# Hedgehog linear attention and an MLP on one core: which engine issues the loads of w1's and w2's later parts, and when

## The chip, the cores and the metric

The kernel runs on one core of one Trainium2 chip. A core has a matrix engine (TensorE, PE in the profile; its weight loads are PEld), a vector engine (VectorE, DVE), an activation engine (ScalarE, ACT), a general engine (GpSimd, POOL) and a small engine that here only issues transfers (SyncE, SP). Each engine works through its own instructions in order. Transfers (DMAs) can be issued by SP, ACT or POOL and are carried out by 16 DMA engines that all of them share. The metric is the device time of one execution in microseconds (us); lower is better.

## The reference

The program is a transformer block of two parts over x of shape 1 x 2048 x 576: linear attention with 32 heads of width 18, then an MLP with 4608 hidden units. All tensors are bf16.

```python
x = A_x
h  = x + _A_ref(_layernorm(x, axis=-1), A_wqkv, A_w_phi, A_wo)
h2 = h + _B_ref(_layernorm(h, axis=-1), B_w1, B_b1, B_w2, B_b2)

# _A_ref: q, k, v = x @ wqkv, by heads
pq = jnp.einsum("bhsd,hdf->bhsf", q, w_phi)      # pk the same from k
phi_q = jnp.concatenate([_softmax(pq, axis=-1), _softmax(-pq, axis=-1)], axis=-1)
kv = jnp.einsum("bhsf,bhsd->bhfd", phi_k, v)
z  = jnp.einsum("bhsf->bhf", phi_k)
num = jnp.einsum("bhqf,bhfd->bhqd", phi_q, kv)
den = jnp.einsum("bhqf,bhf->bhq", phi_q, z)[..., None] + 1e-6
o = num / den                                     # then joined by heads, @ wo

# _B_ref: layernorm once more, then
h = _gelu(jnp.einsum("bsd,df->bsf", y, w1) + b1)
return jnp.einsum("bsf,fd->bsd", h, w2) + b2
```

## The kernel before

The 2048 rows are 16 tiles of 128, taken as 8 pairs (0 to 7). The order of all instructions on all five engines is written out by hand: the calls in the code, from `warm(6)` on, are each engine's order. There is no planner.

**First half.** Keys, values and queries are projected, exponentials of keys are taken on ACT, summed and weighed on DVE and POOL, and `sums(p, a)` (L728) adds every tile's key-value products into one PSUM accumulator, `acc_kv`. The last call is `sums(6, 0)`. After it the tiles `vals` and `exk` (values and weighed key exponentials) are dead, and the memory that they held is given, by `close_keys`, to two weight tiles: w1's second part and w2's first part. So no load of these may start before the last of the sums.

**Weights of the MLP.** w1 (576 x 4608) is held in two parts, one for the steps 0 to 8 of the loop over the hidden layer and one for the steps 9 to 17; `load_w1(q, n, eng)` (L759) loads one sixth of part q, 64 partitions of 3 x 1152 values, 432 KB. w2 (4608 x 576) is held in two parts of 18 blocks of 128 rows; `load_w2(h, n, eng)` (L767) loads one sixth of part h, three blocks, 128 partitions of 3 x 576 values, 432 KB too. The last argument is the engine that issues the load: `syn` is SP, `sca` is ACT, `pool` is POOL. w2's second part lies where the query and value weights were, and may be loaded once the last query product (`query_mm(7, 0)`, L485) is done. w1's first part is loaded much earlier and isn't touched by the change. So 18 loads of 432 KB, 7.96 MB, belong to this place: w1's second part, w2's first part, w2's second part.

**Second half.** Behind the sums the remaining queries are projected, and pair 0 goes through the attention's end: `combine_mm` (query features times `kvm`, L818), `divide` (L831 and L832), a turn by TensorE, the product with wo (`residual_mm`, L868), the layernorms and another turn. Then `first_block` begins. `up` (L1326 on PE, gelu L1348 on ACT) computes the hidden layer of pair 0 in 18 steps, one step giving two blocks of 128 hidden units; steps 0 to 8 read w1's first part, steps 9 to 17 its second. `down` (L1371) multiplies the hidden blocks with w2: for each tile and column half 36 matmuls, j = 0 to 35, counted over the block by k. Even j read w2's first part and odd j the second: matmul j reads block (j - 1) / 2 of the second part, so its sixth number 3 is read first at j = 19, number 4 at j = 25 and number 5 at j = 31.

**What is woven into the first block.** While PE computes `up` for pair 0, POOL and DVE prepare the query features of pair 1: `norm_q(1, i)` sums and weighs them (POOL, L674 and L684) into the two halves of the tile `padded`, and `turn_q(1)` (L713) turns each half into the tile `phit` by a DMA transpose that SP issues. `leave(1)` stands in `down` ahead of matmul k = 2: its `combine_mm` for the two tiles of pair 1 (L818) reads the two halves of `phit`. `norm_q(2, i)` writes into `padded` again and so waits for these transposes.

**Who issues what before the change.** Of w1's second part POOL issues three sixths and SP three; of w2's first part SP issues all six; both are spread from the end of the sums to the end of the written-out list. The six sixths of w2's second part are issued by ACT, one in every second step of `up` (steps 1, 3, 5, 7, 9, 11), each between two gelus. Every DMA that SP or ACT issues also waits, by the program's semaphores, until the one that used the same of eight semaphores before it has landed.

```python
rise = up(0, 1, {
    2 * n + 1: lambda n=n: load_w2(1, n, sca) for n in range(6)
}, 1)
```

Of the kernel before, what the change touches and what calls it, by code (L numbers as in the profile page):

```python
# [47 lines left out]
def kernel(  # L48
# [39 lines left out]
    def take(key):  # L88
        taken[key] = vacant.pop(0)
        return homes[taken[key]][:, :]  # L90

    def leave_home(key):
        vacant.append(taken.pop(key))
# [49 lines left out]
    def region(at, n):  # L143
        return shared[:, at : at + n]
# [214 lines left out]
    pool, vec, syn, sca = nc.gpsimd, nc.vector, nc.sync, nc.scalar  # L359
# [185 lines left out]
    def exponentials(key, dst, p, i):  # L545
        rows = dst[:, :, :].rearrange("p a (h s f) -> p a h s f", s=2, f=DH)
        for s in range(2):
            nc.scalar.activation(  # L548
                rows[:, :, i * HH : (i + 1) * HH, s, :],
                flight[key, p, i][:, :, 0:HALF].rearrange("p a (h f) -> p a h f", f=DH),  # L550
                AF.Exp, scale=1.0 - 2.0 * s,
            )
        give("two", (key, p, i))
# [43 lines left out]
    def query_mm(p, i):  # L597
        features("q", wqp, p, i, CROSSED)

    def query_exp(p, i):  # L600
        if p not in phiq:
            phiq[p] = take(("phiq", p)).rearrange("p (a f) -> p a f", a=2)
        exponentials("q", phiq[p], p, i)
# [97 lines left out]
    def turn_q(p):  # L701
        if p == 0:
            whole = region(4 * PW, 2 * KW * P).rearrange("p (a w k) -> p a w k", a=2, k=P)
            phiT[p] = [whole[:, a, :, :] for a in range(2)]
        elif p in (3, 5):
            phiT[p] = [
                take(("phiT", p, a))[:, 0 : KW * P].rearrange("p (w k) -> p w k", k=P)
                for a in range(2)
            ]
        else:  # L710
            phiT[p] = [phit[:, a, :, :] for a in range(2)]
        for a in range(2):
            nc.sync.dma_start_transpose(phiT[p][a], padded[:, a, :])  # L713
        if p == 0:
            leave_home(("phiq", p))
# [39 lines left out]
    def load_w1(q, n, eng):  # L755
        if q and len(w1) == 1:
            close_keys()
        c0, half = n // 2 * 3, n % 2
        eng.dma_start(  # L759
            w1[q][half * KH : (half + 1) * KH, c0 : c0 + 3, :],  # L760
            w1v[half, :, c0 : c0 + 3, q * FF // 4 : (q + 1) * FF // 4],
        )

    def load_w2(h, n, eng):
        if not w2:
            close_keys()
        eng.dma_start(w2[h][:, 3 * n : 3 * n + 3, :], w2v[h, :, 3 * n : 3 * n + 3, :])  # L767
# [35 lines left out]
    def combine_mm(t, part=None, home=None):  # L803
        p, a = divmod(t, 2)
        if t not in products:
            if home is acc_banks:
                products[t] = home(t)
            else:
                if home:
                    whole = grab("two", ("pn", t), [P, 2, 512], FP32)  # L810
                else:
                    whole = pn_pool.tile([P, 2, 512], FP32, name="pn", tag="pn")
                products[t] = [whole[:, b, :] for b in range(2)]
        pn = products[t]
        for w in range(*((0, KW) if part is None else BANKS[part])):
            b = w // 6
            at, n = (w - BANKS[b][0]) * WV, COUNT[w] * VW
            nc.tensor.matmul(  # L818
                pn[b][:, at : at + n], phiT[p][a][:, w, :], kvm[:, w, 0:n],
                start=True, stop=True,  # L820
            )
        if part != 0 and ("phiT", p, a) in taken:
            leave_home(("phiT", p, a))
# [409 lines left out]
    sums(6, 1)  # L1233
    key_weigh(6, 1, 0, vec)
    sums(6, 0)
    load_w1(1, 0, pool)
    load_w2(0, 2, syn)
    table(0)
    query_mm(7, 1)
    query_exp(7, 1)  # L1240
    combine_mm(1, 0, two)
    table(1)
    combine_mm(1, 1, two)
    divide(1)
    combine_mm(0, 1)
    load_w1(1, 3, syn)
    load_w1(1, 1, syn)
    combine_mm(0, 0)
    query_mm(2, 1)
    query_mm(6, 1)  # L1250
    query_exp(6, 1)
    query_exp(2, 1)
    load_w2(0, 0, syn)
    divide(0)
    turn_o_mm()
    turn_o_ev(1, dve)
    turn_o_ev(0, dve)
    query_mm(3, 1)
    query_exp(3, 1)
    load_w2(0, 3, syn)  # L1260
    load_w2(0, 5, syn)
    residual_mm(0, 0, double_bank(0, 0))
    residual_add(0, 0, 0)
    residual_add(0, 0, 1)
# [2 lines left out]
    residual_add(0, 1, 0)  # L1267
    query_mm(5, 0)
    residual_stats(0, 0, 1)
    load_w1(1, 2, pool)  # L1270
    residual_stats(0, 1, 0)
    residual_add(0, 1, 1)
    query_exp(5, 0)
# [5 lines left out]
    second(1)  # L1279
    query_mm(7, 0)  # L1280
    query_exp(4, 1)
    load_w1(1, 5, syn)
    rescale(0, 0)
    rescale(0, 1)
    turn2_mm(0)
# [3 lines left out]
    copy_b1(act)  # L1289
    rescale(1, 1)  # L1290
    rescale(1, 0)
    load_w2(0, 1, syn)
    load_w1(1, 4, pool)
    load_w2(0, 4, syn)
    gelu_table()
    close_weights()
    hb_pool = side_pool("hb_pool", 1)
# [15 lines left out]
    def up(p0, n, at, first=0):  # L1313
        width = n * TB
        base = p0 % 2 * TB
        per = 2 * PW // width
        h1 = [take(("h1", p0, i)) for i in range((NM + per - 1) // per)]

        def hidden(m):
            return h1[m // per][:, m % per * width : (m % per + 1) * width]  # L1320

        def pair(ph, p_, lo, hi):
            for c in range(KC):
                for half in range(2):
                    rows = slice(half * KH, (half + 1) * KH)
                    nc.tensor.matmul(  # L1326
                        ph[half][:, lo:hi],
                        w1[p_ // 9][rows, c, p_ % 9 * P : (p_ % 9 + 1) * P],
                        ln2T[rows, c, base + lo : base + hi],
                        start=(c == 0), stop=(c == KC - 1),  # L1330
                    )

        def banks_of(p_):
            return [grab("acc", ("h", p0, p_, e), [P, 2 * TB], FP32) for e in range(2)]

        begun = [banks_of(p_) for p_ in range(first)]
        for p_ in range(first):
            pair(begun[p_], p_, 0, P)
            if p_ == 0:
                yield  # L1340
        for p_ in range(NM // 2):
            if p_ in at:
                at[p_]()
            ph = begun[p_] if p_ < first else banks_of(p_)
            pair(ph, p_, P if p_ < first else 0, width)
            for half in range(2):
                m = p_ + half * NM // 2
                nc.scalar.activation(  # L1348
                    hidden(m), ph[half][:, 0:width], AF.Gelu_apprx_tanh,
                    bias=b1col[:, m : m + 1], scale=1.0,  # L1350
                )
                give("acc", ("h", p0, p_, half))
        yield hidden

    def down(p0, n, hidden, at):
        k = 0
        for i_ in range(2 * n):
            t = 2 * p0 + i_
            hb = hb_pool.tile([P, D], FP32, name="hb", tag="hb")
            nc.gpsimd.tensor_tensor(hb[:, :], xh[:, t, :], b2bc[:, :], ALU.add)  # L1360
            ot = tt_pool.tile([P, D], BF16, name="ot", tag="ot")
            last = t == NT - 1
            for c0, c1 in ((0, 512), (512, D)) if last else ((0, HALF), (HALF, D)):
                cs = slice(c0, c1)
                po = grab("acc", ("o", t, c0), [P, c1 - c0], FP32)
                for j in range(NM):
                    m = j // 2 + j % 2 * NM // 2
                    if k in at:
                        at[k]()
                    k += 1  # L1370
                    nc.tensor.matmul(  # L1371
                        po[:, :], hidden(m)[:, i_ * P : (i_ + 1) * P], w2[m // 18][:, m % 18, cs],
                        start=(j == 0), stop=(j == NM - 1),
                    )
                nc.vector.tensor_tensor(ot[:, cs], po[:, :], hb[:, cs], ALU.add)  # L1375
                give("acc", ("o", t, c0))
                if last:
                    nc.sync.dma_start(out_v[:, t, cs], ot[:, cs])
            if not last:
                nc.sync.dma_start(out_v[:, t, :], ot[:, :])  # L1380
        for key in [key for key in taken if key[0] == "h1"]:
            leave_home(key)
# [18 lines left out]
        leave_home(("lnT", i))  # L1401

    def first_block():
        rise = up(0, 1, {
            2 * n + 1: lambda n=n: load_w2(1, n, sca) for n in range(6)
        }, 1)
        turn2_mm(1, pn_pool)
        next(rise)
        for part in range(2):
            turn2_ev(1, part, dve)  # L1410
        for q in (1, 2):
            for i in range(2):
                norm_q(q, i)
            if q == 1:
                turn_q(q)
        down(0, 1, next(rise), {
            2: lambda: (leave(1), turn_q(2)), 66: lambda: enter(1),
            96: lambda: norm_q(3, 0), 112: lambda: leave(2),
        })
# [66 lines left out]
```

## Time and profile before

| | |
|---|---|
| median of 3 executions | 392.45 us (391.16 to 393.12) |
| the profiled execution, own time | 393.02 us |
| its span, first to last instruction | 391.3 us |
| PE busy | 382.6 us, 98% of the span |
| DVE, ACT, POOL busy | 166.2, 162.1, 116.5 us |
| bytes moved by DMA | 35.35 MB |

The profiled execution's own time is 1.7 us more than its span: what lies before the first and behind the last instruction. A row of the timeline gives start, duration, engine, line, operation and tiles, how many instructions it joins (x), and, in brackets, how long the engine had been idle before it and what ended that. The trace calls both weights `w`: L759 is a load of w1, L767 one of w2. `PEq`, `SPq`, `ACTq` are the engines' sequencers, where a DMA is issued; such a row's duration is that of the issue, not of the transfer. The DMA queues are q1 (issued by SP), q10 (issued by ACT) and q0 (issued by POOL).

### The profile page before, as it was taken

Reading aid. Unit: us, or ns where it says so; the run is one execution under the profiler, and the core shown is the slowest. Engines: PE = TensorE matmul, PEld = TensorE weight load, DVE = VectorE, ACT = ScalarE, POOL = GpSimd, SP = SyncE. Lnnn points to the kernel's source line nnn. Section 1 sums busy time; section 2 is a strip of 40 time slices with the busy share of each in tenths; the row PEclk is TensorE's granted clock in tenths of the full one; section 3 lists DMA queues with packets and bytes.
Section 4 is the critical chain, followed back from the end, with each engine's and each line's share of the span. In section 5 each row is a group of like instructions: output and inputs, shape, how many; then the busy total and the mean of one; then the engine's idle time right before and its main releaser. Section 6 shows DMA issues by size and latency. Waiting matters only on the chain.

```text
span 391.3 us, 9949 instructions
## 1 busy us (share of the span) xinstructions
PE 382.6 (98%) x4353; PEld 266.7 (68%) x4354; DVE 166.2 (42%) x362; ACT 162.1 (41%) x290; POOL 116.5 (30%) x159
## 2 busy tenths in 40 slices
PE   8999999999799999999999999999999999999997
PEld 6677878789478887844457887444677764447773
DVE  6999997780249388590029322000480000000100
ACT  4998875698101850056650000666300026661000
POOL 6398995140604653144003111000131110000120
PEclk9999999999899999999999999999999999999999
DMA  7999998999636568533004743000062000000000
GB/s 201 223 206 191 196 219 176 260 256 238 136 60 91 108 106 136 103 67 59 0 2 62 91 106 53 12 1 2 2 88 65 17 17 0 2 2 0 17 31 16
DMA packets 72687, 35.35 MB, mean 90 GB/s; under 512 B 59940, under 2 KB 69860, under 8 KB 72516
## 3 DMA queue, kind: packets, MB, share of 16 engines
q1 hardware_dynamic: 68432, 28.58, 39.8%
q10 hardware_dynamic: 3876, 4.81, 5.2%
q0 software_dynamic: 336, 1.33, 1.3%
q8 instruction: 34, 0.56, 0.6%
q14 instruction: 9, 0.07, 0.1%
HBM read 16.62 MB, written 2.36 MB: 48 GB/s over the span
## 4 chain that ended last, share of the span: by engine, by line
PE 89%; DMA 3%; ACT 2%; issue 2%; DVE 2%; POOL 2%; SPq 1%; POOLq 0%
PE acc L1371 37%; PE acc L1326 31%; PE two L485 9%; PE acc L868 4%; DMA phit<-padded 3%; PE two L511 3%; PE acc_kv L728 1%; POOL padded L674 1%; ACT exk L575 1%; PE two L285 1%; PE acc_kv L276 1%; PE pn L818 1%; SPq L713 1%; DVE ob L832 1%; PE acc L818 0%
## 5 line engine op out<-in xcount | busy, mean ns | idle before, releaser
L1348 ACT ACTIVATE home<-acc,b1col 128x512 bf16<-128x512 f32 (+1 forms) x180 | 98.2, 599 | 173.4 <-PE acc L1326 170.5
L1371 PE MATMUL acc<-w,home 128*128 128x288 bf16 (+2 forms) x1151 | 144.8, 288 | 0.1
L1326 PE MATMUL acc<-shared,w 64*128 64x512 bf16 (+2 forms) x1638 | 142.1, 331 | 0.4 <-ACT home L1348 0.2
L1371 PEld LDWEIGHTS <-home 128*128 128x128 bf16 x1152 | 110.1, 98 | 33.0 <-issue 1.8
L1326 PEld LDWEIGHTS <-w 64*128 64x128 bf16 x1638 | 80.4, 94 | 61.0 <-issue 2.0
L1375 DVE TENSOR_TENSOR ot<-acc,hb 128x288 bf16<-128x288 f32 (+2 forms) x32 | 14.4, 452 | 109.0 <-PE acc L1371 99.1
L1360 POOL TENSOR_TENSOR hb<-xh,b2bc 128x576 f32<-128x576 bf16 x16 | 20.4, 1275 | 104.5 <-DVE ot L1375 104.5
L674 POOL TENSOR_TENSOR padded<-home,rq 128x540 bf16<-128x540 bf16 x32 | 34.9, 1103 | 43.4 <-DMA phit<-padded 20.9
L877 DVE TENSOR_TENSOR xh<-acc,xh 128x288 bf16<-128x288 f32 x28 | 11.4, 447 | 69.9 <-PE acc L868 69.9
L292 POOL TENSOR_TENSOR rs<-va,mhalf 128x1 f32<-128x1 f32 x16 | 8.8, 552 | 102.3 <-DVE va L290 102.3
L485 PEld LDWEIGHTS <-home 64*128 64x128 bf16 x648 | 31.2, 94 | 8.3 <-issue 0.2
L616 POOL TENSOR_TENSOR exk<-exk,rk 128x576 bf16<-128x576 bf16 x20 | 23.6, 1218 | 0.6 <-DVE rk L612 0.6
L548 ACT ACTIVATE home<-two 128x576 bf16<-128x576 f32 x24 | 13.9, 661 | 8.0 <-PE two L485 8.0
L868 PEld LDWEIGHTS <-shared 64*128 64x128 bf16 x288 | 13.8, 94 | 4.4 <-issue 0.5
L296 DVE TENSOR_SCALAR shared<-xh,mv,rs 128x576 bf16<-128x576 bf16 x32 | 16.2, 566 | 0.3 <-DMA shared<-shared 0.3
L868 PE MATMUL acc<-wo,shared 64*128 64x288 bf16 x252 | 16.3, 283 | 0.0
L610 DVE TENSOR_REDUCE sk<-exk 128x64 f32<-128x1152 bf16 x12 | 15.9, 1326 | 0.5 <-ACT exk L548 0.5
L665 DVE TENSOR_REDUCE sk<-home 128x64 f32<-128x1152 bf16 x12 | 15.7, 1310 | 0.0
L831 DVE RECIPROCAL rec<-acc 128x18 f32<-128x18 f32 (+1 forms) x14 | 3.5, 247 | 27.4 <-PE acc L818 27.4
L485 PE MATMUL two<-wqp,home 64*128 64x288 bf16 x216 | 14.4, 283 | 0.0
L485 PE MATMUL two<-wv,home 64*128 64x288 bf16 x216 | 14.4, 283 | 0.0
L548 ACT ACTIVATE exk<-two 128x576 bf16<-128x576 f32 x24 | 13.8, 659 | 1.3 <-PE two L485 1.3
(97 smaller groups left out, 266.7 us busy)
## 6 DMA issues: line engine op xcount, KB each, us to landing
w<-in_B_w_dram SPq DMA_DIRECT2D x12, 432.0 KB, 11.8
w<-in_B_w_dram ACTq DMA_DIRECT2D x9, 432.0 KB, 9.5
out_dram<-ot SPq DMA_DIRECT2D x15, 144.0 KB, 2.1
w<-in_B_w_dram POOLq DMA_DIRECT2D x3, 432.0 KB, 9.8
xh<-in_A_x_dram SPq DMA_DIRECT2D x2, 576.0 KB
xh<-in_A_x_dram SPq DMA_DIRECT2D x3, 288.0 KB, 4.0
wo<-in_A_wo_dram SPq DMA_DIRECT2D x1, 648.0 KB, 5.9
wo<-in_A_wo_dram ACTq DMA_DIRECT2D x1, 648.0 KB, 11.4
```

The source lines that it names most:

```text
L296: nc.vector.tensor_scalar(dst, src, mv[:, i, 0:1], rs[:, i : i + 1], ALU.subtract, ALU.mult)
L485: nc.tensor.matmul(dst[:, a, 0:HALF], lhs[rows, c, :], w[rows, slot, i * HALF : (i + 1) * HALF], start=(n == 0), stop=(n == KC - 1),)
L548: nc.scalar.activation(rows[:, :, i * HH : (i + 1) * HH, s, :], flight[key, p, i][:, :, 0:HALF].rearrange("p a (h f) -> p a h f", f=DH), A ...
L610: nc.vector.tensor_reduce(sk[:, :, :], part_of(dst, i), AX.X, ALU.add)
L616: eng.tensor_tensor(part, part, flight["r" + key, p, i][:, a, :].rearrange("p (h o) -> p h o", o=1).to_broadcast([P, NH, DH]), ALU.mult,)
L665: nc.vector.tensor_reduce(sk[:, :, :], part_of(phiq[p], i), AX.X, ALU.add)
L674: eng.tensor_tensor(padded[:, a, g0 * P : (g0 + 5) * P].rearrange("p (g k) -> p g k", k=P)[:, :, 0:STEP].rearrange("p g (h f) -> p g h f", ...
L868: nc.tensor.matmul(pa[a], oT[p % 2][rows, c, :], wo[rows, c, cs], start=(c == 0), stop=(c == KC - 1),)
L1326: nc.tensor.matmul(ph[half][:, lo:hi], w1[p_ // 9][rows, c, p_ % 9 * P : (p_ % 9 + 1) * P], ln2T[rows, c, base + lo : base + hi], start=(c ...
L1348: nc.scalar.activation(hidden(m), ph[half][:, 0:width], AF.Gelu_apprx_tanh, bias=b1col[:, m : m + 1], scale=1.0,)
L1360: nc.gpsimd.tensor_tensor(hb[:, :], xh[:, t, :], b2bc[:, :], ALU.add)
L1371: nc.tensor.matmul(po[:, :], hidden(m)[:, i_ * P : (i_ + 1) * P], w2[m // 18][:, m % 18, cs], start=(j == 0), stop=(j == NM - 1),)
```

## The change

Three things, all of them about who issues which load and when. No arithmetic, no tile and no matmul is changed, and PE and DVE have the same instructions in the same order.

1. The six loads of w1's second part stand directly behind the sums: numbers 0, 2 and 4 are issued by ACT (number 4 behind the exponentials of query (7, 1)), numbers 1, 3 and 5 by SP. POOL issues none.
2. The six loads of w2's first part are all issued by SP, in a row behind those.
3. The six loads of w2's second part are issued by SP instead of ACT: numbers 0 to 2 ahead of the transposes of `turn_q(1)`, numbers 3 to 5 behind them.

```diff
     sums(6, 0)
-    load_w1(1, 0, pool)
-    load_w2(0, 2, syn)
+    load_w1(1, 0, sca)
+    load_w1(1, 1, syn)
+    load_w1(1, 2, sca)
+    load_w1(1, 3, syn)
+    load_w1(1, 5, syn)
     table(0)
     query_mm(7, 1)
     query_exp(7, 1)
+    load_w1(1, 4, sca)
+    load_w2(0, 0, syn)
+    load_w2(0, 1, syn)
+    load_w2(0, 2, syn)
+    load_w2(0, 3, syn)
+    load_w2(0, 4, syn)
+    load_w2(0, 5, syn)
...
     combine_mm(0, 1)
-    load_w1(1, 3, syn)
-    load_w1(1, 1, syn)
     combine_mm(0, 0)
...
     query_exp(2, 1)
-    load_w2(0, 0, syn)
...
     query_exp(3, 1)
-    load_w2(0, 3, syn)
-    load_w2(0, 5, syn)
...
     residual_stats(0, 0, 1)
-    load_w1(1, 2, pool)
...
     query_exp(4, 1)
-    load_w1(1, 5, syn)
...
     rescale(1, 0)
-    load_w2(0, 1, syn)
-    load_w1(1, 4, pool)
-    load_w2(0, 4, syn)
...
     def first_block():
-        rise = up(0, 1, {
-            2 * n + 1: lambda n=n: load_w2(1, n, sca) for n in range(6)
-        }, 1)
+        rise = up(0, 1, {}, 1)
         turn2_mm(1, pn_pool)
         next(rise)
+        for n in range(3):
+            load_w2(1, n, syn)
         for part in range(2):
             turn2_ev(1, part, dve)
         for q in (1, 2):
             for i in range(2):
                 norm_q(q, i)
             if q == 1:
                 turn_q(q)
+                for n in range(3, 6):
+                    load_w2(1, n, syn)
```

On SP, between the load of b2 and the second pair's attention, the order changes as follows. In these rows `w_1_1518` is w1's second part, `w_0_1519` w2's first part and `w_1_1833` w2's second part.

```order
 L784 DMA b2bc<-in_B_b_dram 128x576
-L767 DMA w_0_1519<-in_B_w_dram 128x3x576
-L759 DMA w_1_1518<-in_B_w_dram 64x3x1152 x2
-L767 DMA w_0_1519<-in_B_w_dram 128x3x576 x3
-L759 DMA w_1_1518<-in_B_w_dram 64x3x1152
-L767 DMA w_0_1519<-in_B_w_dram 128x3x576 x2
+L759 DMA w_1_1518<-in_B_w_dram 64x3x1152 x3
+L767 DMA w_0_1519<-in_B_w_dram 128x3x576 x6
+L767 DMA w_1_1833<-in_B_w_dram 128x3x576 x3
 L713 DMA_TRANSPOSE phit<-padded 128x11x128 x2
+L767 DMA w_1_1833<-in_B_w_dram 128x3x576 x3
 L851 DMA_TRANSPOSE shared<-ob_88 128x9x128
```

Ahead of the two transposes SP had nine loads and now has twelve; three more stand between the transposes and pair 1's own turn (L851).

On ACT, at the end of the sums, the exponentials of the queries (L548) stood in a row; these are its rows before.

```order
L548 ACTIVATE home_71<-two_1353 128x2x16x18 x2
L548 ACTIVATE home_72<-two_1373 128x2x16x18 x2
L548 ACTIVATE home_73<-two_1524 128x2x16x18 x2
L548 ACTIVATE home_70<-two_1597 128x2x16x18 x2
L548 ACTIVATE home_72<-two_1578 128x2x16x18 x2
```

And these are its rows with the change.

```order
L548 ACTIVATE home_71<-two_1353 128x2x16x18 x2
L548 ACTIVATE home_72<-two_1373 128x2x16x18 x2
L759 DMA w_1_1518<-in_B_w_dram 64x3x1152 x2
L548 ACTIVATE home_73<-two_1527 128x2x16x18 x2
L759 DMA w_1_1518<-in_B_w_dram 64x3x1152
L548 ACTIVATE home_70<-two_1605 128x2x16x18 x2
L548 ACTIVATE home_72<-two_1586 128x2x16x18 x2
```

Two issues now stand ahead of the exponentials of query (7, 1) (tile `home_73`), and one behind them. The first of them waits for the last of the sums.

## The prediction

> **What bounds the kernel now.** The page comes first: PE is busy nearly throughout, so only a stretch in which PE waits, or runs slowly, can be won.
>
> ```profile
> PE 382.6 (98%) x4353; PEld 266.7 (68%) x4354; DVE 166.2 (42%) x362; ACT 162.1 (41%) x290; POOL 116.5 (30%) x159
> ```
>
> Second, the table of waits for PE alone: who waited for what, total us, times, longest.
>
> ```profile
> PE pn L818 <- DMA phit<-padded: 2.8, 1, 2.8
> PE pT L379 <- DVE ob L832: 0.3, 1, 0.3
> ```
>
> One wait stands out, for the turned query features of pair 1. Third, PE's timeline from there on, with the same two products for pair 2 further down.
>
> ```profile
> 98.84 0.47 PE L818 MATMUL acc<-kvm,phit 128*128 128x57 bf16 x11
> 102.10 0.56 PE L818 MATMUL pn<-kvm,phit 128*128 128x57 bf16 x11 [2.78 <-DMA phit<-padded]
> 102.49 8.72 PE L1371 MATMUL acc<-w,home 128*128 128x288 bf16 x57
> ...
> 119.96 0.47 PE L818 MATMUL acc<-kvm,phit 128*128 128x57 bf16 x11
> 120.28 0.47 PE L818 MATMUL pn<-kvm,phit 128*128 128x57 bf16 x11
> 120.59 4.08 PE L1371 MATMUL acc<-w,home 128*128 128x288 bf16 x32
> ```
>
> From the first product to the first matmul of `down` behind both it takes 102.49 - 98.84 = 3.65 us here and 120.59 - 119.96 = 0.63 us there: the wait costs **3.02 us**. Fourth, the chain that ended last, and the granted clock in windows (stretch, length, PE busy and PEld busy with counts, clock, DMA share, GB/s; only L1371).
>
> ```profile
> 89.73 12.32 DMA phit<-padded
> 102.05 0.05 issue
> 102.10 0.56 PE pn L818 x11
> 102.66 9.41 PE acc L1371 x64
> ...
> 120.74 3.93 PE acc L1371 x32
> ```
> ```profile
> 102.33:105.74 3.41, 3.25 (x14) 2.13 (x15) 0.50 0.10 20
> 106.00:109.00 3.00, 3.00 (x27) 2.38 (x26) 1.00 1.12 208
> ```
>
> Behind the wait PE runs 3.41 us at half clock; the page's clock row, with slices of 9.8 us, shows nothing of it. 32 matmuls take 3.93 us at full clock, 0.123 each, so the 64 behind the wait would take 7.86 and take 9.41: **1.55 us** more. The wait thus costs 4.57 us in all. The chain as a whole, by engine, is nearly all PE, so what is won here is won at the end.
>
> ```profile
> PE 89%; DMA 3%; ACT 2%; issue 2%; DVE 2%; POOL 2%; SPq 1%; POOLq 0%
> ```
>
> The Trainium skill (TensorE: Matmul & The Clock Gate, section "What's actually happening") has the clock halved after at least one idle window of about 3.4 us, the windows running freely. Here 2.78 us of idleness went ahead of the half clock, less than that window, so the rows set the price. By the Trainium skill alone the half clock need not be this wait's, and only the 3.02 would be won.
>
> **Why the transposes land late.** Issue times on SP, and issue to landing of the two transposes of pair 1 and of the two of pair 2:
>
> ```profile
> 65.60 0.38 SPq L767 DMA_DIRECT2D w<-in_B_w_dram  x1
> 66.07 1.27 SPq L759 DMA_DIRECT2D w<-in_B_w_dram  x2
> 67.40 2.84 SPq L767 DMA_DIRECT2D w<-in_B_w_dram  x3
> 70.28 3.32 SPq L759 DMA_DIRECT2D w<-in_B_w_dram  x1
> 73.64 3.06 SPq L767 DMA_DIRECT2D w<-in_B_w_dram  x2
> 84.86 10.79 SPq L713 DMA_TRANSPOSE phit<-padded  x2
> ```
> ```profile
> DMA to landing us min/median/max: 12.3/13.0/13.7
> ```
> ```profile
> DMA to landing us min/median/max: 3.6/3.7/3.9
> ```
>
> With free DMA engines a transpose takes 3.7 us, here 13. The first, issued at 84.86, landed 13.7 later, at 98.6, just as PE wanted it; the second at 102.05. What they share the engines with, from 92 to 98 us (queue, packets, MB, share of 16 engines):
>
> ```profile
> q10 hardware_dynamic: 1129, 1.25, 85.4%
> q1 hardware_dynamic: 1167, 0.29, 30.4%
> ```
>
> q10 holds ACT's six loads of w2's second part, q1 the transposes. They are issued side by side, and the loads, not needed at once, take four times the bytes. Rates of the stretch:
>
> ```profile
> 66.00:102.00 36.00, 32.61 (x578) 28.50 (x572) 18.99 (x43) 26.55 (x57) 9.13 (x12) 1.00 1.05 244
> 70.00:76.00 6.00, 6.00 (x97) 4.81 (x99) 3.75 (x12) 3.94 (x8) 0.00 (x0) 1.00 0.98 261
> 98.00:102.00 4.00, 1.31 (x22) 0.70 (x17) 1.41 (x4) 1.15 (x3) 1.10 (x1) 1.00 1.00 204
> ```
>
> The DMA engines are full (share 1.05) from 66 to 102 us: 36 x 244 = 8.78 MB, of which 18 loads of 0.442 MB are 7.96 and two transposes (128 x 1408 values of 2 bytes, 0.36 MB) 0.72. The change can't make this less; it changes **the order** in which it is served.
>
> **The change part by part.** *The queue.* Three of ACT's six loads now stand behind the transposes, so ahead of their end there are 15 loads and the two, 6.63 + 0.72 = 7.35 MB. The old stretch landed 8.68 MB between the first issue at 65.60 and 102.05, 4.20 us a MB with all latencies. At that pace the transposes are in at 65.6 + 30.9 = 96.5 us and the last three loads at 98.3, 100.2 and 102.05. PE wants the transposes at 98.8 and 99.2: 2.3 us to spare. Without the wait `down` resumes at 98.84 + 0.63 = 99.47 with k = 2, and reaches w2's last three sixths (j = 19, 25, 31) after 17, 23 and 29 matmuls of 0.123: at 101.6, 102.3 and 103.0. The margins are 3.3, 2.1 and 1.0 us. So nothing waits, and 4.57 us go.
>
> Bounds of the pace: the fast end is 261 GB/s, where everything is in earlier. At the slow end, 204 throughout and 1.6 us of latency (the first load needed 3.4 from issue to landing, by the row below, and 1.8 is its share at 244), the transposes land at 65.6 + 1.6 + 36.0 = 103.2, and w2's last sixth at 109.7. I take the whole stretch's own pace, since bytes and engines are the same.
>
> ```profile
> DMA to landing us min/median/max: 3.4/11.6/17.1
> ```
>
> *SP's issues.* A load's issue takes 0.6 us (1.27 for two), but stalls when the queue is full: at 70.28 one took 3.32. By 76.70 SP had issued nine loads, and until 77 q1 had moved 1.81 MB, 4.1 of them; so the queue takes about five.
>
> ```profile
> q1 hardware_dynamic: 1249, 1.81, 58.5%
> ```
>
> SP issues its twelfth load when seven of its own and ACT's three are through: ten, 4.42 MB, at 65.6 + 18.6 = 84.2. The features of pair 1 come at 84.83 and 87.2:
>
> ```profile
> 82.41 2.16 POOL L674 TENSOR_TENSOR padded<-home,rq 128x540 bf16<-128x540 bf16 x2 [4.39 <-DVE rq L657]
> 84.54 0.29 POOL L684 TENSOR_TENSOR padded<-home,rq 128x72 bf16<-128x72 bf16 x1
> ```
>
> The transposes are thus ready when SP is. A delay of SP of a few us costs nothing while the queue ahead still drains. Behind SP's last three issues stands pair 1's own turn, due only when `divide` is done behind both products, and not read until k = 66, 64 matmuls or 7.9 us after k = 2, twice a transpose's 3.7. The new wait of the first transpose, by its semaphore, is for the eighth load back, and ten are through by then.
>
> *ACT's three issues* take 0.62 us each (half the 1.27) and stand in two idle stretches:
>
> ```profile
> 66.70 1.20 ACT L548 ACTIVATE home<-two 128x576 bf16<-128x576 f32 x2 [2.76 <-PE two L485]
> 69.74 1.74 ACT L548 ACTIVATE home<-two 128x576 bf16<-128x576 f32 x3 [1.85 <-PE two L485]
> ```
>
> SP's first load, which waits for the last of the sums too, went out at 65.60; so ACT's first two are out by 66.85, 0.15 past the exponentials' old start, and the 1.85 us idle behind take that up with the third. I take 0. Nothing gains by them; the loss is at most 2.1 us, if the third stalls as SP's did (3.32 less the 1.2 left of the idle stretch). *Taken from ACT in the rise*: six issues, of 0.37 us, between gelus that ran on at the same spacing with and without one: 0.
>
> ```profile
> 85.77 0.37 ACTq L767 DMA_DIRECT2D w<-in_B_w_dram  x1
> 86.05 2.07 ACT L1348 ACTIVATE home<-acc,b1col 128x256 bf16<-128x256 f32 x4
> 87.74 0.37 ACTq L767 DMA_DIRECT2D w<-in_B_w_dram  x1
> ```
>
> *Taken from POOL*: three issues; it waits for DVE ahead of the features of pair 1 (4.39 us, above), so 0.
>
> On a stall of ACT behind SP the Trainium skill (Perfetto Trace Analysis, section "DMA Instruction — HWDGE (DVE, Sync)") lets the two issuing sequencers share one descriptor generator that each locks. By the Trainium skill's rule ACT could stand still while SP stalls. The rows above speak against it: ACT's issue at 85.77 took 0.37 us while SP's transposes were stuck from 84.86 to 95.65.
>
> **Sum.** 393.02 - 3.02 - 1.55 = 388.45 us against the profiled execution. That lies 0.57 above the median of the three; with the same step the median becomes 392.45 - 4.57 = 387.9. I say **388.0**.
>
> **The rivals.** (a) *The tail is late*: the transposes come in time, but w2's last sixths hold up `down` for 0.5 to 3 us, in pieces or too briefly for the clock. For it: a margin of only 1.0 us; 0.1 us a load more takes 1.8 off it. Against: the rate was worst while two queues mixed. Time 388.4 to 391. A fifth of its chance is the half clock that stays although the wait goes: 392.45 - 3.02 = 389.4. That is what the Trainium skill's clock gate rule, taken alone, would give. (b) *The wait stays or only moves*: the transposes still land past 101, PE idles over 2 us again and the half clock follows, so under 1 us is won, 391.5 to 393; or ACT stalls by its 2.1 us, 387.9 + 2.1 = 390.0. (c) *Slower*: SP's single queue doesn't keep the rate, and the last sixth comes later than the old `down` reached it. That was 107.6 us (102.49, plus 29 matmuls of 0.123 and the 1.55), so it decides where 8.68 MB take more than 107.6 - 65.6 - 1.6 = 40.4 us, below 215 GB/s; at the 204 above, w2's last sixth is in at 109.7, and the time is 2.1 us over the old one, 394.6. Against it: from 76 to 82 us q1 alone carried nearly everything, at 256.
>
> ```profile
> 76.00:82.00 6.00, 5.92 (x118) 5.01 (x114) 4.96 (x11) 5.74 (x11) 1.74 (x3) 1.00 1.08 256
> ```
>
> **How the numbers follow.** Forecast 0.60 (387.2 to 388.8), (a) 0.19, (b) 0.12, (c) 0.09. What a measurement of this kernel can tell from no change is about 0.5%, 2.0 us: below 390.5 lie the forecast and two thirds of (a), 0.73; between, the rest of (a), (b) and a little of (c), 0.19; above 394.4 the rest of (c), 0.08. The range that leaves out two in ten reaches from 387.0 to 391.4, through (a) and a part of (b).
>
> **What would show it.** Right: PE's row at L818 without a bracket, no stretch at 0.50 clock near 102, the transposes 7 to 12 us from issue to landing but in by 98.8, q10 empty after 80. Wrong: a wait of PE on `w` in `down` (a), still one on `phit` (b), exponentials that start past 70 (ACT's stall), or under 215 GB/s between 66 and 102 (c).

## The result and the profile after

| | before | after |
|---|---|---|
| median | 391.92 us (390.63 to 393.12, 6 executions) | 388.34 us (388.14 to 389.15, 6 executions) |
| the profiled execution, own time | 393.02 us | 388.26 us |
| its span | 391.3 us | 386.5 us |

The ratio is 0.9913, 95% interval 0.9888 to 0.9937: 0.9% faster, 3.6 us by the medians and 4.8 by the two profiled executions. 388.0 was forecast. Here and below, the ratios leave out executions that took over 1.5% more than the fastest of the same kernel, while medians and ranges count them all.

PE's timeline of the changed kernel, at the place where the wait was:

```profile
98.88 0.47 PE L818 MATMUL acc<-kvm,phit 128*128 128x57 bf16 x11
99.20 0.47 PE L818 MATMUL pn<-kvm,phit 128*128 128x57 bf16 x11
99.51 8.00 PE L1371 MATMUL acc<-w,home 128*128 128x288 bf16 x64
```

No bracket stands behind the second product any more, and from the first product to `down` it takes 0.63 us instead of 3.65. PE came there at 98.88, where it had come at 98.84, so nothing ahead of it was lost or won. In the chain that ended last the transposes are gone, and the 64 matmuls behind take 7.85 us where they took 9.41:

```profile
99.35 0.32 PE pn L818 x11
99.67 7.85 PE acc L1371 x64
```

The issues on SP (start, duration, count) show the new order, and the transposes' times from issue to landing are half of what they were:

```profile
65.78 1.93 SPq L759 DMA_DIRECT2D w<-in_B_w_dram  x3
67.82 15.68 SPq L767 DMA_DIRECT2D w<-in_B_w_dram  x9
85.11 6.38 SPq L713 DMA_TRANSPOSE phit<-padded  x2
91.53 1.64 SPq L767 DMA_DIRECT2D w<-in_B_w_dram  x3
```
```profile
DMA to landing us min/median/max: 5.8/6.5/7.1
```

The two were issued at 85.11 and 89.19, so they landed at 92.2 and 95.0; the last load of w2 was in at 98.5. In the windows (stretch and length; busy time and count of PE, PEld, DVE, ACT and POOL; granted clock, DMA share, GB/s), the bytes from 66 to 102 us are the same 8.8 MB, but they are moved sooner:

```profile
66.00:102.00 36.00, 35.30 (x612) 31.10 (x609) 20.38 (x48) 26.42 (x57) 12.02 (x15) 1.00 0.91 244
82.00:88.00 6.00, 5.69 (x103) 5.32 (x99) 5.81 (x7) 5.70 (x15) 4.82 (x6) 1.00 1.10 360
98.00:102.00 4.00, 4.00 (x58) 3.24 (x53) 2.61 (x8) 1.33 (x4) 2.14 (x3) 1.00 0.00 0
```

From 82 to 88 us, with w2's loads alone in SP's queue, the engines carry 360 GB/s; before, no window of the prediction had more than 261. From 98 us on they stand idle.

### The profile page after: what moved, and what is told of

Its sections match the earlier page's. It is cut to its first block, busy times and chain, and to the rows that moved or that the text cites. A ratio compares the mean times of both kernels' runs of the same rounds, so it can differ in the third digit from the quotient of the medians.

```text
span 386.5 us, 9946 instructions
## 1 busy us (share of the span) xinstructions
PE 380.5 (98%) x4353; PEld 265.9 (69%) x4354; DVE 166.3 (43%) x362; ACT 161.7 (42%) x290; POOL 114.3 (30%) x156
## 4 chain that ended last, share of the span: by engine, by line
PE 93%; ACT 3%; DMA 2%; DVE 1%; issue 0%; SPq 0%
PE acc L1371 37%; PE acc L1326 36%; PE two L485 10%; PE acc L868 4%; PE two L511 3%; PE acc_kv L728 1%; DMA w<-in_A_wqkv_dram 1%; ACT exk L575 1%; DMA xh<-in_A_x_dram 1%; PE acc L818 1%; PE two L868 1%; PE pn L818 1%; DVE ob L832 1%; PE two L447 0%; ACT home L412 0%; ACT L931 0%
## 5 line engine op out<-in xcount | busy, mean ns | idle before, releaser
L1371 PE MATMUL acc<-w,home 128*128 128x288 bf16 (+2 forms) x1151 | 143.2, 286 | 0.1
L1326 PE MATMUL acc<-shared,w 64*128 64x512 bf16 (+2 forms) x1638 | 141.9, 331 | 0.4 <-ACT home L1348 0.2
L1326 PEld LDWEIGHTS <-w 64*128 64x128 bf16 x1638 | 80.4, 94 | 60.7 <-issue 1.8
L548 ACT ACTIVATE home<-two 128x576 bf16<-128x576 f32 x24 | 13.8, 661 | 8.1 <-PE two L485 4.9
L548 ACT ACTIVATE exk<-two 128x576 bf16<-128x576 f32 x24 | 13.7, 660 | 1.3 <-PE two L485 1.3
```

Source lines behind the costliest of these rows:

```text
L548: nc.scalar.activation(rows[:, :, i * HH : (i + 1) * HH, s, :], flight[key, p, i][:, :, 0:HALF].rearrange("p a (h f) -> p a h f", f=DH), A ...
L1326: nc.tensor.matmul(ph[half][:, lo:hi], w1[p_ // 9][rows, c, p_ % 9 * P : (p_ % 9 + 1) * P], ln2T[rows, c, base + lo : base + hi], start=(c ...
L1371: nc.tensor.matmul(po[:, :], hidden(m)[:, i_ * P : (i_ + 1) * P], w2[m // 18][:, m % 18, cs], start=(j == 0), stop=(j == NM - 1),)
```

## The experiments

Two questions were open. First, which part of the change took the wait away. The prediction's account is **order**: three loads go behind the transposes instead of beside them. Its rival is **rate**: loads in a row are carried faster, wherever the last three stand. Second, whether the half clock is the wait's doing.

**The third part alone.** The kernel before, in which only w2's second part is moved to SP.

```diff
-        rise = up(0, 1, {
-            2 * n + 1: lambda n=n: load_w2(1, n, sca) for n in range(6)
-        }, 1)
+        rise = up(0, 1, {}, 1)
...
+        for n in range(3):
+            load_w2(1, n, syn)
...
+                for n in range(3, 6):
+                    load_w2(1, n, syn)
```

> The kernel before with the third part of the change alone: w2's second part issued by SyncE, three sixths ahead of the second pair's transposes and three behind, while w1's second part and w2's first part stay where they were. Theory O (order: the transposes only have to be ahead of the last three loads in one queue): they land by about 97 us, TensorE doesn't wait, no half clock, 388.3 us, 3.6 less than before. Theory R (rate: loads in a row and without GpSimd's queue are carried faster, and that is what won the time): the rate stays at some 244 GB/s, and the wait for the transposes stays, over 2 us, at 391 to 392 us.

389.02 us (388.36 to 391.21, 10 executions), the kernel before beside it 394.45 (390.26 to 400.18, 27); ratio 0.9923, 95% interval 0.9886 to 0.9959. PE at the two products:

```profile
99.03 0.47 PE L818 MATMUL acc<-kvm,phit 128*128 128x57 bf16 x11
99.35 0.47 PE L818 MATMUL pn<-kvm,phit 128*128 128x57 bf16 x11
99.67 1.51 PE L1371 MATMUL acc<-w,home 128*128 128x288 bf16 x11
```

No wait: the third part is enough in this execution. The second transpose landed at 97.6, which leaves less margin than the 95.0 with all three parts. Two of the ten executions took over 391 us, at a granted clock of 0.999 and more, so without a half clock; what cost them isn't shown.

**Without the third part.** The changed kernel with ACT's six loads in the rise again (the same lines the other way round).

> The changed kernel without its third part: w2's second part is issued by ScalarE between the gelus again, while w1's second part and w2's first part go out in a row at the end of the sums. Theory O: the transposes share the engines with ScalarE's six loads again and land at 100 to 102 us; wait of 1 to 3 us, half clock with it, 390 to 392 us. Theory R: everything is in by about 98.5 us, no wait, 388.3 us.

390.81 us (388.96 to 395.04, 10); ratio 0.9940, interval 0.9907 to 0.9973. Its profile has both the wait and the half clock:

```profile
83.20 15.06 PE L1326 MATMUL acc<-shared,w 64*128 64x256 bf16 x267 [0.22 <-ACT home L1348]
99.38 0.39 PE L1326 MATMUL acc<-shared,w 64*128 64x256 bf16 x3 [1.12 <-issue]
99.70 0.42 PE L1371 MATMUL acc<-w,home 128*128 128x288 bf16 x2
99.96 0.47 PE L818 MATMUL acc<-kvm,phit 128*128 128x57 bf16 x11
101.89 0.70 PE L818 MATMUL pn<-kvm,phit 128*128 128x57 bf16 x11 [1.47 <-DMA phit<-padded]
```
```profile
101.22:104.63 3.41, 2.73 (x21) 1.95 (x22) 1.98 (x6) 0.00 (x0) 2.65 (x4) 0.50 0.17 51
```

So earlier loads of w1 and w2 don't remove the wait, although a ratio under 1 says that they win something too; order was favoured by these two runs. But a second idle time appears, 1.12 us inside a step of the rise, that neither account had.

**All six ahead.** The changed kernel, with no load behind the transposes.

```diff
-        for n in range(3):
+        for n in range(6):
             load_w2(1, n, syn)
...
-                for n in range(3, 6):
-                    load_w2(1, n, syn)
```

> The changed kernel with all six loads of w2's second part ahead of the transposes on SyncE, none behind. Theory O at the pace of the old stretch (4.2 us a MB): the transposes are last, land at about 102 us, wait near 3 us and half clock, 392 us. Theory R: at the changed kernel's own rate three loads more take 3.7 us, the transposes land at 98.7 instead of 95.0, just when TensorE wants them: wait under 0.3 us, 388.3 to 388.7 us.

388.63 us (388.31 to 389.29, 6); ratio 0.9908, interval 0.9876 to 0.9939. All 18 loads are ahead of the transposes, and the second still landed at 99.12, with PE's product at 99.33:

```profile
99.01 0.47 PE L818 MATMUL acc<-kvm,phit 128*128 128x57 bf16 x11
99.33 0.47 PE L818 MATMUL pn<-kvm,phit 128*128 128x57 bf16 x11
```
```profile
88.00:92.00 4.00, 4.00 (x78) 4.00 (x74) 0.04 (x1) 3.43 (x9) 0.00 (x0) 1.00 1.07 353
92.00:98.00 6.00, 6.00 (x114) 6.00 (x111) 0.00 (x0) 5.14 (x13) 0.02 (x1) 1.00 1.29 171
95.00:98.00 3.00, 3.00 (x60) 3.00 (x56) 0.00 (x0) 2.57 (x7) 0.02 (x1) 1.00 1.33 156
```

Order falls: the half that stands behind the transposes needn't stand there. Rate foretold this run (98.7 us) but not the one before it, where the wait stayed. The first run and this one have in common that ACT issues none of w2's second part. That gave a third account, **mixing**: loads of another queue, in flight beside the transposes, drag both.

**The last three by ACT.** The changed kernel, in which the same three loads that go behind the transposes are issued by ACT in the rise.

```diff
-        rise = up(0, 1, {}, 1)
+        rise = up(0, 1, {
+            2 * n - 1: lambda n=n: load_w2(1, n, sca) for n in range(3, 6)
+        }, 1)
...
-                for n in range(3, 6):
-                    load_w2(1, n, syn)
```

> The changed kernel with one difference: the last three sixths of w2's second part are issued by ScalarE between gelus, in steps 5, 7 and 9 of the rise, instead of by SyncE behind the transposes. The same bytes are ahead of the transposes in SyncE's queue; three loads run beside them in the other queue. Theory M (loads of another queue beside the transposes drag both, and delay TensorE's instructions too): transposes in at 98 us or later instead of 95.0, rate under 120 GB/s in some 2 us of 88 to 98, half of the runs with a wait; median 389 to 391 us. Theory B (only the bytes ahead count): at most the three loads, 3.7 us, come between, shared: transposes in by 97 us, no wait, 388.3 us.

391.90 us (390.40 to 393.74, 10), the kernel before beside it 393.56 (390.79 to 400.56, 14); ratio 0.9967, interval 0.9932 to 1.0003. Three loads in the other queue give most of the gain back: the changed kernel beside it took 388.36. In its profiled execution a half clock follows the waits, as in the kernel before. The transposes' issue to landing, the windows, and PE:

```profile
DMA to landing us min/median/max: 12.4/13.7/14.9
```
```profile
84.00:88.00 4.00, 3.69 (x65) 3.43 (x64) 3.93 (x5) 3.86 (x11) 4.00 (x5) 1.00 1.09 355
88.00:92.00 4.00, 4.00 (x79) 4.00 (x76) 0.75 (x2) 3.42 (x9) 0.33 (x2) 1.00 1.43 222
92.00:98.00 6.00, 6.00 (x115) 6.00 (x111) 0.00 (x0) 5.13 (x14) 0.00 (x0) 1.00 1.11 187
98.00:102.00 4.00, 2.05 (x35) 1.51 (x30) 0.00 (x0) 1.58 (x5) 0.98 (x1) 1.00 1.10 174
```
```profile
101.31 0.39 PE L1326 MATMUL acc<-shared,w 64*128 64x256 bf16 x3 [1.95 <-issue]
101.63 0.42 PE L1371 MATMUL acc<-w,home 128*128 128x288 bf16 x2
101.89 0.47 PE L818 MATMUL acc<-kvm,phit 128*128 128x57 bf16 x11
103.07 0.68 PE L818 MATMUL pn<-kvm,phit 128*128 128x57 bf16 x11 [0.71 <-DMA phit<-padded]
```
```profile
103.13:106.54 3.41, 3.41 (x24) 2.36 (x25) 2.00 (x6) 0.00 (x0) 3.38 (x4) 0.50 0.01 2
```

Up to 88 us the rate is that of the changed kernel, 355 GB/s. From 92 to 102 the transposes and ACT's loads run side by side, at 174 to 187 GB/s; the transposes land at 100.9 and 103.0 instead of 92.2 and 95.0. With all six ahead in SP's queue, the three loads went first at 353, and the transposes behind them were in at 97.8 and 99.1. The low rate alone is no proof: in that run the transposes alone, all that was left from 95 to 98 us, were carried at 156. The proof is the end: the same bytes and the same transposes took until 103.0 in two queues and until 99.1 in one. Of these 3.9 us, 0.7 are older, since this execution's rise began later (84.30 against 83.56); the other 3.1 are mixing. These landings are of one profile each, and this one is of the slowest of the ten executions; but the fastest of the ten, 390.40, is still above all four of the changed kernel beside it, 388.58 at most. Mixing is so shown for loads issued by ACT; why two queues end later than one is open.

**The changed kernel and the kernel before, once more.**

> The changed kernel once more, beside the others on one chip: no wait for the transposes, no half clock, no stop of TensorE inside a step of the rise; 388.3 to 389 us with a spread of about 1 us.

> The kernel before once more, for a second profile. If its spread of several us comes from TensorE running out of instructions while the DMA engines are jammed, this profile shows idle time of TensorE inside a step of the rise, at loads that wait for nothing, at the 84th, 212th or 340th weight load of it (128 apart), and the transposes landing at 102 us or later.

The changed kernel took 388.36 us (388.22 to 388.58, 4), ratio 0.9863, interval 0.9818 to 0.9908; its profile has neither wait nor stop. The kernel before took 390.82 in its profiled execution:

```profile
83.25 8.20 PE L1326 MATMUL acc<-shared,w 64*128 64x256 bf16 x139 [0.22 <-ACT home L1348]
92.13 7.38 PE L1326 MATMUL acc<-shared,w 64*128 64x256 bf16 x131 [0.68 <-issue]
99.44 0.42 PE L1371 MATMUL acc<-w,home 128*128 128x288 bf16 x2
99.69 0.47 PE L818 MATMUL acc<-kvm,phit 128*128 128x57 bf16 x11
101.54 0.48 PE L818 MATMUL pn<-kvm,phit 128*128 128x57 bf16 x11 [1.38 <-DMA phit<-padded]
```
```profile
101.00:104.00 3.00, 2.46 (x29) 2.04 (x30) 1.94 (x6) 0.00 (x0) 2.37 (x3) 1.00 0.00 0
```

The transposes landed at 101.5, a little ahead of the 102 that was expected. The stop came where it was expected: 139 matmuls into this row, and in the two kernels above 267 into it, 128 apart. A matmul comes with a weight load, so that is 256 instructions, and the matmuls at these places wait for nothing in the program's order. The profile's instruction queue (q8) moves blocks of 16 KB (34 packets, 0.56 MB, in the kernel before), which is 64 bytes for each of 256. That PE had run out of instructions, whose block came late through the same engines, fits all of this, but it is argued and not shown: no run changed the instruction loading by itself. And here the wait of 1.38 us was not followed by a half clock.

**The wait filled.** The kernel before, with 40 matmuls on the identity ahead of the second product; their output is overwritten.

```diff
         pn = products[t]
+        if t == 3:
+            for _ in range(40):
+                nc.tensor.matmul(pn[0][:, 0:P], ident[:, :], ident[:, :], start=True, stop=True)
```

> The kernel before with 40 idle matmuls of 128 columns (0.056 us each, 2.2 us) on TensorE in the wait for the second transpose; their output is overwritten. If the half clock is the wait's doing, it goes, and the 1.55 us with it: 390.4 us against 391.9, the transpose landing at 102 as before. If the half clock has another cause: 391.9 us, or a little more if the matmuls outlast the wait.

393.17 us (391.51 to 398.99, 10) against 394.45; ratio 0.9994, interval 0.9953 to 1.0034: no difference that can be told, so the 1.55 us were not won. On the cause of the half clock the profile says this (its lines stand three further down: L1329 is the kernel's L1326, and L817 are the added matmuls):

```profile
93.69 7.41 PE L1329 MATMUL acc<-shared,w 64*128 64x256 bf16 x131 [1.50 <-issue]
...
101.60 2.39 PE L817 MATMUL pn<-ident 128*128 128x128 bf16 x40
104.08 0.48 PE L821 MATMUL pn<-kvm,phit 128*128 128x57 bf16 x11
```
```profile
104.00:106.00 2.00, 1.92 (x25) 1.60 (x26) 1.33 (x4) 0.00 (x0) 1.84 (x2) 1.00 0.00 0
```

The second transpose came at 104.0, after a stop of 1.50 us in the rise, and the clock stayed at 1.00 all the way. One profile can't settle it, since the kernel before had none in its second profile either. The granted clocks of all executions say more. One half clock of 3.41 us lowers the mean over a span of 391.3 us to 1 - 0.5 x 3.41 / 391.3 = 0.996, and the profile before, with one, has 0.996. Of the 10 executions with the wait filled, 9 have 0.999 or more; of the 27 of the kernel before beside them, 4. Of the changed kernel, all 10 have 1.00. So PE's idle time there brings the half clock about. That filling it wins nothing may lie in the filler, whose 2.39 us can be longer than the wait (1.38 in the second profile); fewer matmuls were not tried.

**w1's loads by SP alone.** The stretch's rate is uneven, so two runs ask whether w1's sixths, each of which fills 64 partitions, are the slow part: grouped by partitions as below, or alternating, in the order 0 to 5.

```diff
-    load_w1(1, 0, sca)
-    load_w1(1, 1, syn)
-    load_w1(1, 2, sca)
-    load_w1(1, 3, syn)
-    load_w1(1, 5, syn)
+    load_w1(1, 0, syn)
+    load_w1(1, 2, syn)
+    load_w1(1, 4, syn)
+    load_w1(1, 1, syn)
+    load_w1(1, 3, syn)
+    load_w1(1, 5, syn)
```

> The changed kernel with w1's second part issued by SyncE alone, the three sixths for partitions 0 to 63 first and then the three for 64 to 127; nothing else. Theory H (a load into 64 partitions moves at about half the rate of w2's 128-partition loads, some 175 GB/s, unless the other half moves too): the stretch from 67 to 80 us stays near 175 GB/s, w1 is in at about 81 to 82 us and the second transpose at about 97 to 98. Otherwise (the slower rate at first is the start of two queues): 230 GB/s or more from 67 to 80, transpose at 95 or earlier. Time 388.3 us in both cases, since TensorE needs neither before.

> As the run with w1's sixths grouped by partitions, but in the order 0 to 5, so that sixths for partitions 0 to 63 and for 64 to 127 alternate in SyncE's queue. Theory H: little better than grouped if one load is served after the other, 175 to 220 GB/s; 300 or more if the halves overlap. Time 388.3 us.

389.37 and 388.35 us, one execution each; the kernel before beside them took 390.21. From 67 to 79 us the rates were 189 and 217 GB/s (the first row, then the second), against 255 in the changed kernel with halves on two queues:

```profile
67.00:79.00 12.00, 11.69 (x199) 9.05 (x197) 8.93 (x29) 7.35 (x13) 1.11 (x2) 1.00 0.95 189
...
67.00:79.00 12.00, 11.69 (x198) 9.05 (x197) 9.11 (x26) 8.05 (x14) 1.12 (x2) 1.00 1.02 217
```

The transposes landed at 99.0 and 97.5, still in time. w1's loads are thus the slow ones, at roughly 200 GB/s where w2's reach 355; with two queues they had 255, in one execution. The grouped kernel started its loads 0.8 us later than the other. Whether the 64 partitions or another property of these loads makes them slow was not tried.

## Why the prediction came out

**The wait, 3.02 us, and the half clock, 1.55 us.** Both terms were right for the profiled execution: the rows after give 3.65 - 0.63 = 3.02 and 9.41 - 7.85 = 1.56, of the 4.76 between the profiled executions; the last 0.2 us lie in no row that I can name. The median fell by 3.6, not 4.6: not every execution of the kernel before has the half clock, nor a wait of 2.78 us, as its second profile shows (a wait of 1.38 and no half clock). That the forecast of 388.0 is within 0.34 of the measured median is in part luck: the step of 4.57 was 1.0 us more than the medians fell, and the median that it was taken from, 392.45, was 0.5 more than that of six executions, 391.92.

The Trainium skill (TensorE: Matmul & The Clock Gate, section "What's actually happening") has free-running windows of about 3.4 us. The half clock lasted 3.41 us each of the three times and came or didn't with the same kind of wait, which agrees. It asks for one idle window; here a window that was partly idle was enough. In the 3.41 us ahead of the half clock, PE was idle for 2.78 us in the kernel before, for 2.30 with the last three loads by ACT (1.59 of the stop and the wait of 0.71), and for 1.92 without the third part (1.12 and the first 0.80 of the wait, as the half clock began at 101.22). After 1.38 and 1.50 us, in the second profile before and with the wait filled, it did not come.

**The queue.** This is the step whose reason failed: "Three of ACT's six loads now stand behind the transposes, so ahead of their end there are 15 loads and the two", and "the change can't make this less; it changes the order". With all 18 loads ahead there is no wait either, and with 15 ahead and three beside, there is. What matters in these runs is that none of ACT's loads runs beside the transposes. The bytes stay, but the time that they take does not: 4.20 us a MB was the pace of a stretch with several queues, and with the change the same 8.68 MB took 98.5 - 65.8 = 32.7 us, 3.77 us a MB. The forecast landings of 96.5 and 102.05 us became 95.0 and 98.5, and the transposes took 5.8 and 7.1 us where 7 to 12 were forecast. A share over 1 was also misread as engines that are full: it counts the time of packets, and in the kernel before next to nothing was moved at a share of 1.17.

```profile
96.30:97.50 1.20, 1.20 (x28) 1.20 (x24) 0.00 (x0) 0.91 (x4) 0.00 (x0) 1.00 1.17 19
```

The effect was right because one queue removes the mixing and sets the order at once.

**SP's issues.** The twelfth load was to be issued at 84.2 and was out at 83.5 (67.82 + 15.68). The first transpose was issued when its data was ready, at 85.11, the second only at 89.19, because the first one's issue took 3.96 us; its data was ready at 87.5.

**ACT's issues**, costed at 0. The exponentials of query (7, 1) began at 67.38 instead of 66.70, 0.68 us later where 0.15 was forecast, and the next at 69.94 instead of 69.74. PE came to `down` within 0.04 us of before: nothing was lost.

**The rivals.** (a), a late tail, did not come: the last sixth was in 4.5 us ahead of PE. (c) did not come either. (b), a wait that stays, is what the kernel with three loads on ACT shows, at 391.9. The price for ACT's six issues in the rise, 0, holds for their time on ACT; their loads, in flight beside the transposes, are what made the wait. The stops in the rise came only with them too.

## What to carry to other kernels

Where a DMA transpose is due, look at what the other queues have in flight beside it, not only at what stands ahead of it: all 18 loads ahead of it cost nothing here, three beside it cost 3.5 us. Don't take a DMA share over 1 for engines that carry all they can; look at the GB/s beside it. A rate measured in a stretch with several queues is no constant to forecast a new order with. And a wait of a few us on TensorE should be looked up in windows of the granted clock, since it can cost half as much again behind it, in some executions and not in others.

## What the runs showed of the hardware that was not expected

- Transposes beside three loads of ACT's queue ended at 103.0 us, and behind the same loads in SP's queue at 99.1. Of the difference, 0.7 us are a later start. Loads of w2 alone in SP's queue ran at 353 to 360 GB/s, transposes alone behind them at 156 over 3 us, and both beside each other at 174 to 187 over 10 us. The Trainium skill (DMA: Bandwidth & Descriptors, section "Issuing engines are not separate DMA queues") lets the choice of the issuing engine save only the time to issue. Here three loads moved from one to the other made 3.5 us of difference (388.36 to 391.90), so the measurement speaks against it where transposes run beside.
- TensorE stopped for 0.68 to 1.95 us inside a step, at places 256 instructions apart, in four of the five profiles with ACT's loads beside the transposes; in the six without, the table of waits shows no such stop. The cause is open.
- The executions of the kernel before that the ratios count spread over 390.3 to 395.7 us, those of the changed kernel over 388.1 to 389.2. The half clocks are a part of that spread: on one chip the four executions without one took 390.3 to 390.9.
